# Queue order between attention and the first expert of a fused attention, mixture and SwiGLU kernel

## Chip, core and metric

The kernel runs on one core of a Trainium2 chip. The time is the device time of one execution in microseconds (us). The core has five engines that run beside each other, each from a queue of its own and in the order of that queue: TensorE (PE, matmuls and transposes into PSUM), VectorE (DVE), ScalarE (ACT), GpSimd (POOL, here mostly scatters to DRAM by computed row numbers) and SyncE (SP, here the queue that issues nearly all DMAs). An instruction waits for semaphores of other engines and of DMAs, and while it waits nothing behind it in its queue starts.

## What is computed

```python
attn = softmax(q k^T / 8 + slope[h] * -(i - j), masked to 0 <= i - j < 128) @ v   # 4 x 8 heads, 576 rows, 64 wide
x = attn as 2304 tokens x 512
logits = x @ w_gate + log1p(exp(x @ w_noise)) * noise                             # 8 experts
top2, top2_w = two largest logits of a token, softmax over the two
out[token] = sum over its two experts: top2_w * (relu(x @ w1[e]) @ w2[e])         # 512 -> 1024 -> 512
xn = out / rms(out) * rms_g
result = (silu(xn @ w_gate2) * (xn @ w_val)) @ w_out                              # 512 -> 1536 -> 512
```

## The kernel before

All arithmetic on PE that matters for precision is split: a float32 weight or activation becomes a float16 high part and a float16 rest, and three products replace one. A weight is split by an ACT instruction (the high part, L128, scaled) and a DVE instruction (the rest, L130), after a DMA of 512 KB has brought the float32 piece into one of four `st` buffers (L110).

**Attention.** The main loop counts `n`, one step for each pair of heads: 18 token tiles of 128 rows, four steps each, so n = 0 to 71, and some steps of run-out. A step issues the scores of n + 2 (L342), transposes of the probabilities of n, the product with v of n - 2. When a tile is complete, `split_x` makes its float16 halves `x16` (the high half on DVE L426, the rest on POOL L428, for the last tile on DVE), and `put_x` turns it into `xTg`: by a DMA transpose (L434) up to tile 14, by PE transposes (L438) and an ACT copy (L439) for tiles 15 to 17. `logits(t)` (L502) multiplies it with the gate weights. `route` then works on batches of tiles (0 to 2, 3 to 5, 6 to 9, 10 to 13, 14 and 15, 16 and 17): softplus on ACT (L512, L513), the top two on DVE, their rank by two small matmuls (L539, L541), and `slots` (L560), the row of each token in its expert's list. `scatter` sends the two copies of a tile's `x16` to `xrows` in DRAM by one indirect DMA each from POOL (L483), with a small memset ahead.

**Experts.** `row_steps` brings 128 rows of an expert's list back by a DMA transpose on SP (`xT`, L171). Expert 0 starts before the routing has ended: its first 256 rows when tiles 0 to 9 are routed, the next 128 after tile 13, and `LAST`, rows 384 to 639, after tile 17. `first_steps` is the hidden layer: for each of eight chunks f, 12 matmuls into a PSUM buffer (L187; names mm0, three buffers, and mm1, two), then ACT writes `hh` (L192) and DVE `hl` (L193), which frees the buffer. `second_steps` is the output layer, 24 matmuls of 512 columns a tile into `acc` (L208, two buffers), which ACT empties into `ys` (L230) for a DMA to `ybuf`. A generator yields after each six matmuls with the columns that PE has done.

**What sets the order.** Inside `manual_schedule` an engine's queue stands as the code is written. In the kernel before, this holds up to n = 75. From n = 76 up to the call of `drive` for expert 0 a scheduler of the framework orders the queues. From there on the order is by hand again: `drive` walks over PE's steps, counts columns, and calls a side generator when its due column is reached: `(start, period, generator)`. `weight_steps(e)` is such a generator: eight loads of 512 KB (four of w1, four of w2), each split in two halves. In the attention loop the loads and splits for expert 0 are called by a list of n. For expert 1 three loads stand directly ahead of `drive`.

```python
    drive(itertools.chain(exp0, expert_steps(0, LAST)),
          (0, 500, row_steps(0, LAST)), (0, 3000, weights0), (0, 3000, weights1),
          *((6000 + 6000 * i, 500, row_steps(1, cs)) for i, cs in enumerate(HALVES)),
          (40000, 4000, mix()), (58000, 5000, ahead(2)))
```

After expert 7 follow the combination, the norm and SwiGLU.

## Time and profile before

| | |
|---|---|
| three runs, median (lowest to highest) | 1026.11 us (1024.42 to 1030.59) |
| the profiled execution | 1031.71 us, of which the span from first to last instruction 1030.0 us |
| PE busy | 965.4 us, 94% of the span, 7184 matmuls |
| DVE, ACT, POOL busy | 685.8, 452.9, 215.2 us |
| mean granted clock of PE | 0.976 of full speed |
| chain that ended last, by engine | PE 70%, DMA 9%, DVE 9%, POOL 4% |

A share of the whole span says little here, since the program has stages with different limits: attention up to about 200 us, the hand-over to the experts up to about 250 us, experts to about 640 us, SwiGLU to the end. Times below are us from the start of the span.

### The profile page before, as it was taken

Reading aid. Unit: us, or ns where it says so; the run is one execution under the profiler, and the core shown is the slowest. Engines: PE = TensorE matmul, PEld = TensorE weight load, DVE = VectorE, ACT = ScalarE, POOL = GpSimd, SP = SyncE. Lnnn points to the kernel's source line nnn. Section 1 sums busy time; section 2 is a strip of 40 time slices with the busy share of each in tenths; the row PEclk is TensorE's granted clock in tenths of the full one; section 3 lists DMA queues with packets and bytes.
Section 4 is the critical chain, followed back from the end, with each engine's and each line's share of the span. In section 5 each row is a group of like instructions: output and inputs, shape, how many; then the busy total and the mean of one; then the engine's idle time right before and its main releaser. Section 6 shows DMA issues by size and latency. Waiting matters only on the chain.

```text
span 1030.0 us, 18541 instructions
## 1 busy us (share of the span) xinstructions
PE 965.4 (94%) x7184; PEld 672.3 (65%) x7184; DVE 685.8 (67%) x1584; ACT 452.9 (44%) x936; POOL 215.2 (21%) x261
## 2 busy tenths in 40 slices
PE   7898878869999999999999998889999999999997
PEld 4787777555565656565656577468658848857874
DVE  7788767533767666666666468998818936863750
ACT  6787766333445454545453244433422422341320
POOL 3446552600000000000000236652230150130000
PEclk9999998989999999999999999899999999999999
DMA  9999994783948584848582032302150151122000
GB/s 234 203 228 226 261 265 113 246 203 124 221 160 218 166 222 160 230 158 224 164 226 81 21 92 83 66 28 82 27 138 2 32 123 43 31 58 57 1 11 34
DMA packets 178560, 135.52 MB, mean 132 GB/s; under 512 B 130976, under 2 KB 148128, under 8 KB 178464
## 3 DMA queue, kind: packets, MB, share of 16 engines
q1 hardware_dynamic: 172704, 115.38, 44.3%
q0 software_dynamic: 5760, 18.88, 6.0%
q8 instruction: 58, 0.95, 0.4%
q14 instruction: 38, 0.31, 0.1%
HBM read 76.81 MB, written 26.74 MB: 101 GB/s over the span
## 4 chain that ended last, share of the span: by engine, by line
PE 70%; DMA 9%; DVE 9%; POOL 4%; issue 3%; ACT 3%; SPq 2%; ACTq 0%; DVEq 0%; POOLq 0%
PE mm L1045 20%; PE acc L208 19%; PE mm L187 18%; PE acc L972 11%; DMA raw<-in_qkv 3%; DVE sums L996 3%; POOL xrows L483 2%; DMA st<-in_moe_w 2%; DMA xTg<-x 1%; DMA xq<-xg 1%; DMA kqT<-kq 1%; POOL kq L267 1%; DVE ss L354 1%; SPq L901 1%; PE mm L342 1%
## 5 line engine op out<-in xcount | busy, mean ns | idle before, releaser
L187 PE MATMUL mm<-xT,w1h 128*128 128x256 f16 (+2 forms) x1088 | 167.2, 294 | 9.2 <-DVE hl L193 9.2
L187 PEld LDWEIGHTS <-w1h 128*128 128x128 f16 x1088 | 104.9, 99 | 48.6 <-issue 10.0
L193 DVE SCALAR_TENSOR_TENSOR hl<-mm,hh 128x256 f16<-128x256 f32 (+2 forms) x136 | 63.4, 469 | 104.4 <-ACT hh L192 102.6
L208 PE MATMUL acc<-w2h,hh 128*128 128x512 f16 x320 | 122.1, 382 | 0.0
L208 PE MATMUL acc<-w2l,hh 128*128 128x512 f16 x320 | 122.0, 381 | 0.0
L208 PE MATMUL acc<-w2h,hl 128*128 128x512 f16 x320 | 121.8, 381 | 0.0
L1002 POOL TENSOR_TENSOR sw<-sums,sw 128x256 f16<-128x256 f32 x36 | 28.5, 810 | 395.6 <-ACT sw L999 395.6
L208 PEld LDWEIGHTS <-hh 128*128 128x128 f16 x640 | 62.9, 98 | 72.9 <-ACT hh L192 0.6
L1045 PE MATMUL mm<-xq,sw 128*128 128x256 f16 x864 | 100.4, 273 | 1.7 <-DMA xq<-xg 1.7
L187 PE MATMUL mm<-xT,w1l 128*128 128x256 f16 (+2 forms) x544 | 92.7, 293 | 0.0
L1045 PEld LDWEIGHTS <-sw 128*128 128x128 f16 x864 | 84.4, 98 | 12.1 <-issue 2.0
L192 ACT ACTIVATE hh<-mm 128x256 f16<-128x256 f32 (+2 forms) x136 | 56.2, 418 | 80.2 <-PE mm L187 75.6
L972 PE MATMUL acc<-oh__3438,pgl 128*128 128x512 f16 (+2 forms) x228 | 84.5, 373 | 2.9 <-DVE pgl L954 2.9
L972 PE MATMUL acc<-oh__3438,pgh 128*128 128x512 f16 (+2 forms) x228 | 84.4, 372 | 0.2 <-ACT pgh L952 0.2
L972 PE MATMUL acc<-ol__3439,pgh 128*128 128x512 f16 (+2 forms) x228 | 84.3, 372 | 0.0
L972 PEld LDWEIGHTS <-pgh 128*128 128x128 f16 x456 | 44.4, 99 | 50.7 <-issue 2.2
L363 ACT ACTIVATE pr<-ss,nm 128x256 f32<-128x256 f32 (+1 forms) x144 | 63.1, 487 | 25.2 <-DVE nm L354 23.8
L187 PEld LDWEIGHTS <-w1l 128*128 128x128 f16 x544 | 52.7, 99 | 18.1
L354 DVE CUSTOM_DVE_ANT_0 ss<-mm,bias 128x256 f32<-128x256 f32 (+1 forms) x144 | 54.1, 396 | 11.4 <-PE mm L342 6.7
L371 PE MATMUL mm<-ident,pr 128*128 128x128 f32 x272 | 47.8, 293 | 14.0 <-DVE rs L416 8.8
L230 ACT ACTIVATE ys<-acc 128x512 f32<-128x512 f32 x40 | 23.7, 593 | 84.6 <-PE acc L208 68.6
L1054 DVE TENSOR_TENSOR gt<-mm,p 128x512 f32<-128x512 f32 x24 | 16.6, 690 | 60.7 <-PE mm L1045 58.6
(208 smaller groups left out, 1937.3 us busy)
## 6 DMA issues: line engine op xcount, KB each, us to landing
st<-in_moe_w SPq DMA_DIRECT2D x64, 512.0 KB, 5.0
ybuf<-ys SPq DMA_DIRECT2D x40, 256.0 KB, 2.0
raw<-in_qkv SPq DMA_DIRECT2D x17, 512.0 KB, 5.0
st<-in_moe_w_gate SPq DMA_DIRECT2D x12, 512.0 KB, 5.4
st<-in_moe_w_val SPq DMA_DIRECT2D x12, 512.0 KB, 4.9
st<-in_moe_w_out SPq DMA_DIRECT2D x12, 512.0 KB, 5.3
v<-in_qkv SPq DMA_DIRECT2D x18, 279.0 KB, 4.8
out<-ys SPq DMA_DIRECT2D x17, 256.0 KB, 2.2
```

The lines of the kernel that those rows point to most:

```text
L187: nc.tensor.matmul(hp[:, :w], w1[:, c, f * P:(f + 1) * P], xT[:, xo + c, cs], start=(n == 0), stop=(n == 3 * KC - 1))
L192: nc.scalar.activation(hh[:, f, hs], hp[:, :w], AF.Relu)
L193: nc.vector.scalar_tensor_tensor(hl[:, f, hs], hp[:, :w], 0.0, hh[:, f, hs], op0=OP.max, op1=OP.subtract)
L208: nc.tensor.matmul(yp, hx[:, f, i * P:(i + 1) * P], w2[:, f, :], start=(n == 0), stop=(n == 3 * FC - 1))
L230: nc.scalar.activation(ys, yp, AF.Copy, scale=YSC)
L354: nc.vector.tensor_tensor_reduce(out=d["ss"][:, j, c0:], in0=d["sp"][:, j, c0:], in1=bias[kind][:, 2 * d["hp"] + j, c0:], scale=-1.0 / KS, ...
L363: nc.scalar.activation(d["pr"][:, j, c0:], d["ss"][:, j, c0:], AF.Exp, scale=-1.0, bias=d["nm"][:, j:j + 1])
L371: nc.tensor.transpose(pt[:, j, kk, :], d["pr"][:, j, kk * P:(kk + 1) * P], ident)
L972: nc.tensor.matmul(op[:, ds], px[:, f, cs], w[:, f, ds], start=(k == 0), stop=(k == 3 * GC - 1))
L996: nc.vector.tensor_tensor(out=o, in0=x, in1=y, op=op)
L1002: nc.gpsimd.tensor_tensor(out=here[k][1], in0=x, in1=here[k][0], op=OP.subtract)
L1045: nc.tensor.matmul(pp, w(a, pa, c), xq[:, 4 * b + 2 * pb + c, :], start=(n == 0), stop=(n == 5))
```

## The change

The order is now by hand from the start of the loop to the end: `order.close()` at n = 76 is gone, and the steps of the run-out are written so that the queues stand as wanted. In its parts:

- `weight_steps` issues load i when the second half of piece i - 3 comes up, which is behind the split that last read the `st` buffer that it will fill. Before, it stood one half-step earlier.
- The batch of tiles 10 to 13 (`t0 = 10`) loses three pauses in `route` and is done three steps of n earlier. From n = 68 two scatters are issued in a step (before: from n = 77).
- The last tile is divided, split and turned one step earlier, its `logits` comes at n = 75 (before: 76), and the splits of expert 0's w2 are put behind that work (before: from n = 72 on).
- Expert 0 takes its first 256 and its next 128 rows through the hidden layer and then all three tiles through the output layer (before: hidden and output layer of the 256, then of the 128).
- The three loads for expert 1 ahead of `drive` are gone. Inside it, both transposes of `LAST` come at column 0, expert 1's weights from column 9000 every 2500 (before 0 and 3000), its rows from 14000 (before 6000).

```diff
@@ weight_steps
-        for i in range(len(srcs) + 3):
-            if i < len(srcs):
-                src = srcs[i]
-                sts.append(stage.tile([P, FE], F32, name="st").rearrange("p (a d) -> p a d", a=src.shape[1]))
-                nc.sync.dma_start(sts[i], src)
-            if i < 3:
-                yield
-                continue
...
+        def load():
+            src = srcs[len(sts)]
+            sts.append(stage.tile([P, FE], F32, name="st").rearrange("p (a d) -> p a d", a=src.shape[1]))
+            nc.sync.dma_start(sts[-1], src)
+
+        for _ in range(3):
+            load()
+            yield
...
+        for k, j in itertools.product(range(len(srcs)), range(2)):
+            if j and len(sts) < len(srcs):
+                load()
...
@@ drive
-                    next(s[2], None)
+                    if next(s[2], s) is s:
+                        break
@@ route (three places)
-            if t0 < 11:
+            if t0 < 10:
                 yield
@@ the loop over n
-        exp0 = itertools.chain(*(expert_steps(0, cs) for cs in EARLY.values()))
+        exp0 = expert_steps(0, *EARLY.values())
...
-            if n == 76:
-                order.close()
...
-            if n % 2 == 0 and HP <= n < NS + HP:
+            if n % 2 == 0 and HP <= n < NS + 2:
                 parts.append(divide((n - HP) // HP, (n - HP) // 2 % 2))
+            if n == NS + 1:
+                parts.append(divide(NT - 1, 1))
...
-                for _ in range(1 if n < 77 else 2):
-                    next(exp0, None)
+                next(exp0, None)
...
-            if p == (3 if NT - 6 <= t - 1 < NT - 1 else 2) and 1 <= t <= NT:
+            if p == (1 if t == NT else 3 if NT - 6 <= t - 1 < NT - 1 else 2) and 1 <= t <= NT:
                 split_x(t - 1)
...
-            if p == 3 and 1 <= t <= NT:
+            if p == (2 if t == NT else 3) and 1 <= t <= NT:
                 put_x(t - 1)
-            if n in (HP * NT + 1, HP * NT + 4) or p == 0 and 3 <= t < NT + 1:
-                r = {HP * NT + 1: NT - 2, HP * NT + 4: NT - 1}.get(n, t - 3)
+            if n in (NS + 1, NS + 3) or p == 0 and 3 <= t < NT + 1:
+                r = {NS + 1: NT - 2, NS + 3: NT - 1}.get(n, t - 3)
...
-                scatter(1 if n < 77 else 2)
-
-            for _ in range((n in (50, 53, 56, 58, 60, 62, 64, 66, 68, 70)) + (n in (72, 73) or n >= 76) * 2):
+                scatter(1 if n < 68 else 2)
+
+            if n in (50, 53, 56, 58, 60, 62, 64, 66, 68, 70, 72) or n > NS + 3:
                 next(weights0, None)
@@ ahead of drive for expert 0, and its call
-    for _ in range(3):
-        next(weights1)
...
-    order.enter_context(tc.manual_schedule())
...
-          (0, 500, row_steps(0, LAST)), (0, 3000, weights0), (0, 3000, weights1),
-          *((6000 + 6000 * i, 500, row_steps(1, cs)) for i, cs in enumerate(HALVES)),
+          (0, 0, row_steps(0, LAST)), (0, 1600, weights0), (9000, 2500, weights1),
+          *((14000 + 6000 * i, 500, row_steps(1, cs)) for i, cs in enumerate(HALVES)),
```

From expert 1's own matmuls on, the queues of all five engines hold the same instructions in the same order as before. Three places show what moves. Line numbers of the changed kernel differ by up to 3.

POOL's queue at the end of attention, before (x16_3047 is tile 16, x16_2048 and x16_2200 are tiles 10 and 11, whose scatters follow):

```order
L428 TENSOR_TENSOR x16_2744<-x_2628,x16_2744 128x512
L428 TENSOR_TENSOR x16_2895<-x_2773,x16_2895 128x512
L428 TENSOR_TENSOR x16_3047<-x_2937,x16_3047 128x512
L482 MEMSET apart_171 1x1
L483 DMA xrows_76<-x16_2048,slots_79 18432x1024
```

The same place after (x16_3065 is tile 16, x16_2411 and x16_2589 are tiles 12 and 13; the memset and the second scatter of each tile are left out):

```order
L431 TENSOR_TENSOR x16_2897<-x_2771,x16_2897 128x512
...
L486 DMA xrows_76<-x16_2048,slots_79 18432x1024
...
L486 DMA xrows_76<-x16_2200,slots_79 18432x1024
...
L486 DMA xrows_76<-x16_2411,slots_79 18432x1024
L431 TENSOR_TENSOR x16_3065<-x_2941,x16_3065 128x512
...
L486 DMA xrows_76<-x16_2589,slots_79 18432x1024
```

The rest of tile 16 (L428, now L431) stood ahead of all scatters of tiles 10 to 13, and now stands behind six of them.

SP's queue at the hand-over, before (xT_2794 are rows of expert 0, xT_3475 of expert 1; st_3428 to st_3432, st_3452 and st_3471 are expert 1's first five loads, st_3120 is expert 0's last; TENSOR_LOAD and ISA read a flag, and the x2 below them are the two transposes of `LAST`):

```order
L110 DMA st_3120<-in_moe_w2 128x2x512
L110 DMA st_3428<-in_moe_w1 128x4x256
L110 DMA st_3430<-in_moe_w1 128x4x256
L110 DMA st_3432<-in_moe_w1 128x4x256
L171 DMA_TRANSPOSE xT_2794<-xrows_76 128x8x128
L1157 TENSOR_LOAD over_82
L1157 ISA x2
L171 DMA_TRANSPOSE xT_2794<-xrows_76 128x8x128 x2
L110 DMA st_3452<-in_moe_w1 128x4x256
L231 DMA ybuf_77<-ys_3461 128x512
L110 DMA st_3471<-in_moe_w2 128x2x512
L171 DMA_TRANSPOSE xT_3475<-xrows_76 128x8x128 x3
```

The same place after (xT_2795 are rows of expert 0, xT_3506 of expert 1; st_3340 is expert 0's last load, st_3447 and the loads below it are expert 1's):

```order
L174 DMA_TRANSPOSE xT_2795<-xrows_76 128x8x128
L111 DMA st_3340<-in_moe_w2 128x2x512
L1156 TENSOR_LOAD over_82
L1156 ISA x2
L174 DMA_TRANSPOSE xT_2795<-xrows_76 128x8x128 x2
L111 DMA st_3447<-in_moe_w1 128x4x256
L111 DMA st_3472<-in_moe_w1 128x4x256
L111 DMA st_3504<-in_moe_w1 128x4x256
L174 DMA_TRANSPOSE xT_3506<-xrows_76 128x8x128 x3
L111 DMA st_3560<-in_moe_w1 128x4x256
```

All eight loads of expert 1 now stand behind the two transposes of `LAST` (five before), which wait for the last scatter.

ACT's queue where the hidden layer of `LAST` begins, before (w2h_3456 is expert 1's weight, st_3608 its last piece; hh_3680 is `LAST`):

```order
L128 ACTIVATE w2h_3456<-st_3542 128x512 x2
L230 ACTIVATE ys_3677<-acc_3644 128x512
L748 ACTIVATE cd_3441<-cd_3441 128x18
L192 ACTIVATE hh_3680<-mm0_3682 128x256
L128 ACTIVATE w2h_3456<-st_3608 128x512
L192 ACTIVATE hh_3680<-mm1_3701 128x256
```

The same place after (w1h_3533 and w2h_3535 are expert 1's weights, acc_3553, acc_3599 and acc_3643 the three output tiles of expert 0's first 384 rows, hh_3684 is `LAST`):

```order
L130 ACTIVATE w1h_3533<-st_3504 128x4x128 x2
L233 ACTIVATE ys_3596<-acc_3553 128x512
L130 ACTIVATE w1h_3533<-st_3560 128x4x128 x2
L130 ACTIVATE w2h_3535<-st_3574 128x512 x2
L130 ACTIVATE w2h_3535<-st_3592 128x512
L748 ACTIVATE cd_3372<-cd_3372 128x18
L233 ACTIVATE ys_3640<-acc_3599 128x512
L130 ACTIVATE w2h_3535<-st_3592 128x512
L130 ACTIVATE w2h_3535<-st_3614 128x512 x2
L130 ACTIVATE w2h_3535<-st_3626 128x512 x2
L233 ACTIVATE ys_3681<-acc_3643 128x512
L195 ACTIVATE hh_3684<-mm0_3686 128x256
```

All sixteen splits of expert 1's weights now stand ahead of the first `hh` of `LAST`. Before, the last two stood between its first ones.

## Rows read from the trace of the kernel before

**Rows 1.** Windows of 50 us: busy us and instructions by engine, clock, DMA share, GB/s.

```profile
150.00:200.00 50.00, 37.97 (x378) 30.64 (x376) 33.82 (x145) 25.46 (x55) 18.94 (x32) 0.86 0.66 189
200.00:250.00 50.00, 40.82 (x296) 26.48 (x295) 15.90 (x38) 15.01 (x37) 3.25 (x3) 0.90 0.69 169
250.00:300.00 50.00, 50.00 (x303) 29.42 (x301) 35.18 (x62) 23.97 (x47) 0.00 (x0) 1.00 0.67 181
```

**Rows 2.** Timeline of PE: start, us, instruction, idle time before it and its releaser.

```profile
158.72 0.28 PE L502 MATMUL rt<-wgh,xTg 128*128 128x16 f16 x4 [7.42 <-DMA xTg<-x]
...
174.74 0.73 PE L438 MATMUL mm<-ident,x 128*128 128x128 f16 x8
...
176.23 0.60 PE L187 MATMUL mm<-xT,w1h 128*128 128x256 f16 x4
...
177.54 0.25 PE L502 MATMUL rt<-wgh,xTg 128*128 128x16 f16 x4
...
193.23 0.25 PE L502 MATMUL rt<-wgh,xTg 128*128 128x16 f16 x4
...
216.37 0.58 PE L187 MATMUL mm<-xT,w1h 128*128 128x128 f16 x4 [6.78 <-DVE hl L193]
...
223.52 0.60 PE L187 MATMUL mm<-xT,w1h 128*128 128x256 f16 x4
...
232.64 0.94 PE L187 MATMUL mm<-xT,w1h 128*128 128x256 f16 x4 [2.40 <-DVE hl L193]
```

**Rows 3.** The chain that ended last, in order of time: start, us, what.

```profile
203.09 3.42 DMA xrows<-x,slots
...
228.58 1.15 ACT w2h L128 x2
...
238.39 10.36 PE acc L208 x48
```

**Rows 4.** Timeline of ACT at the start of the last rows of expert 0.

```profile
230.22 0.37 ACT L192 ACTIVATE hh<-mm 128x256 f16<-128x256 f32 x1
```

**Rows 5.** Timeline of SP, which issues the DMAs: start, us that the issue took.

```profile
146.29 0.81 SPq L110 DMA_DIRECT2D st<-in_moe_w  x1
147.21 3.55 SPq L434 DMA_TRANSPOSE xTg<-x  x1
...
165.56 18.71 SPq L110 DMA_DIRECT2D st<-in_moe_w  x6
...
230.67 1.65 SPq L110 DMA_DIRECT2D st<-in_moe_w  x3
```

**Rows 6.** Windows as in Rows 1, of four stretches.

```profile
150.00:155.00 5.00, 1.30 (x13) 1.14 (x10) 2.44 (x9) 0.98 (x3) 0.00 (x0) 0.92 1.24 313
160.00:165.00 5.00, 5.00 (x37) 4.71 (x36) 3.21 (x20) 3.38 (x9) 0.00 (x0) 0.55 0.58 123
...
206.50:230.50 24.00, 16.96 (x152) 12.62 (x150) 7.54 (x18) 7.35 (x22) 0.00 (x0) 0.86 0.94 208
232.00:237.50 5.50, 4.86 (x30) 3.72 (x30) 3.17 (x9) 1.49 (x5) 0.00 (x0) 0.69 0.91 285
```

**Rows 7.** Timeline of DVE: step 69, then the slots of two batches.

```profile
171.70 0.08 DVE L354 DVE_READ_ACCUMULATOR2_ANT nm<- 128x1 f32 x1
...
176.60 0.21 DVE L557 TENSOR_TENSOR oh<-oh,rt 128x64 f32<-128x64 f32 x1
...
177.10 0.17 DVE L560 SCALAR_TENSOR_TENSOR slots<-chosen,rank 128x8 int32<-128x8 f32 x1
...
196.72 0.16 DVE L560 SCALAR_TENSOR_TENSOR slots<-chosen,rank 128x4 int32<-128x4 f32 x1
```

**Rows 8.** Timeline of POOL: tile 16's rest, first and seventh scatter behind it.

```profile
173.87 1.16 POOL L428 TENSOR_TENSOR x<-x,x 128x512 f16<-128x512 f32 x1 [6.11 <-DVE x L426]
...
177.54 0.98 POOL L483 DMA_INDIRECT xrows<-x,slots  x1 [2.48 <-DVE rank L562]
...
186.28 0.96 POOL L483 DMA_INDIRECT xrows<-x,slots  x1 [0.22 <-issue]
```

More of the change, by code (lines that the diff above doesn't have):

```diff
@@ L105, in weight_steps @@
         sts, last = [], None
-        for i in range(len(srcs) + 3):
-            if i < len(srcs):
-                src = srcs[i]
-                sts.append(stage.tile([P, FE], F32, name="st").rearrange("p (a d) -> p a d", a=src.shape[1]))
-                nc.sync.dma_start(sts[i], src)
-            if i < 3:
-                yield
-                continue
-            if i == 3:
-                ws += [wpool.tile([P, KC, FE], F16, name="w1h"), wpool.tile([P, KC, FE], F16, name="w1l"),
-                       wpool.tile([P, FC, DM], F16, name="w2h"), wpool.tile([P, FC, DM], F16, name="w2l")]
-            k = i - 3
-            for j in range(2):
-                fs = slice(j * n // 2, (j + 1) * n // 2)
-                if k < 4:
-                    st = sts[k][:, :, fs]
-                    hi, lo = (w[:, :, k * n + fs.start:k * n + fs.stop] for w in ws[:2])
-                else:
-                    st = sts[k][:, j:j + 1]
-                    hi, lo = (w[:, (k - 4) * m + j:(k - 4) * m + j + 1] for w in ws[2:])
-                scale = SW1 if k < 4 else SW2
-                nc.scalar.activation(hi, st, AF.Copy, scale=scale)
-                if last:
-                    nc.vector.scalar_tensor_tensor(*last, op0=OP.mult, op1=OP.subtract)
-                last = lo, st, scale, hi
-                yield
@@ new lines, in load @@
+        def load():
[5 more added lines that the diff above has]
+            yield
+        ws += [wpool.tile([P, KC, FE], F16, name="w1h"), wpool.tile([P, KC, FE], F16, name="w1l"),
+               wpool.tile([P, FC, DM], F16, name="w2h"), wpool.tile([P, FC, DM], F16, name="w2l")]
+        for k, j in itertools.product(range(len(srcs)), range(2)):
+            if j and len(sts) < len(srcs):
+                load()
+            fs = slice(j * n // 2, (j + 1) * n // 2)
+            if k < 4:
+                st = sts[k][:, :, fs]
+                hi, lo = (w[:, :, k * n + fs.start:k * n + fs.stop] for w in ws[:2])
+            else:
+                st = sts[k][:, j:j + 1]
+                hi, lo = (w[:, (k - 4) * m + j:(k - 4) * m + j + 1] for w in ws[2:])
+            scale = SW1 if k < 4 else SW2
+            nc.scalar.activation(hi, st, AF.Copy, scale=scale)
+            if last:
+                nc.vector.scalar_tensor_tensor(*last, op0=OP.mult, op1=OP.subtract)
+            last = lo, st, scale, hi
+            yield
@@ L534, in route @@
             yield
-            if t0 < 11:
+            if t0 < 10:
                 yield
@@ L554, in route @@
             yield
-            if t0 < 11:
+            if t0 < 10:
                 yield
```

## The prediction

> **What bounds the kernel now.** First the windows of 50 us. From 250 us on PE is busy 50.00 of 50 us [rows 1], and the queues there stand as before, so a change can come only from the stretch before. Between 150 and 250 us PE is busy 37.97 + 40.82 = 78.8 of 100 us: 21.2 us of idle time are all that there is to win, with what the clock takes. The timeline of PE tells where they lie [rows 2]: 7.42 us up to 158.72, where `logits` of tile 13 waits for its DMA transpose `xTg`; 6.78 us up to 216.37 and 2.40 us up to 232.64, where the hidden layer of expert 0 waits for `hl`. Behind an idle time the granted clock is low: 0.55 between 160 and 165 us [rows 6].
>
> Who is late in the second half is seen in the chain that ended last, read forwards [rows 3]: the last scatter is issued at 203.09 and lands at 206.51. Only then can SP turn the rows of `LAST`, and all loads behind that in SP's queue come later still. The chain ends with two splits of expert 1's w2 on ACT at 228.58, right behind a load; the first `hh` of `LAST` follows at 230.22 [rows 4]; PE starts again at 232.64 and ends expert 0 at 238.39 + 10.36 = 248.75. So from 206.51 to 232.64 the hand-over is paced by transfers and by ACT's queue behind them, and PE fills in. Whatever the change does, the end of expert 0 follows from two numbers: when the last scatter lands, and how long the transfers ahead of `LAST`'s first `hh` then take.
>
> **The change part by part.** *A load behind a transpose.* Load 3 of expert 0 is issued at 146.29, directly ahead of tile 13's `xTg` at 147.21 [rows 5], for which PE waits 7.42 us. It now stands behind it. The load is 128 x 4 x 256 x 4 bytes = 0.524 MB; at the 313 GB/s of 150 to 155 us [rows 6] that is 1.7 us. Bounds: 0, if the scatters fill the place (the DMA share is 1.24 there), and 2.5 at the 208 GB/s of the later stretch [rows 6]. I take -1.7, the row of the place itself. For experts 2 to 7 the same edit changes no row of SP's queue: nothing.
>
> *The batch of tiles 10 to 13 earlier.* Its `slots` now stand directly behind the maxima of step 69, which end at 171.78; from L557 at 176.60 to the end of `slots` at 177.27 the work takes 0.67 us [rows 7]. So they come at 171.78 + 0.67 - 1.7 = 170.75, 6.5 us earlier than before. But POOL's queue has six of the eight scatters ahead of tile 16's rest. The first scatter started 0.27 us behind `slots`, the seventh 8.74 us behind the first (177.54, 186.28) [rows 8]: 170.75 + 0.27 + 8.74 = 179.8, plus 1.16 for the rest [rows 8] = 180.9. PE wants it for the second half of tile 16's transposes at 174.74 + 0.36 - 1.7 = 173.4 [rows 2]. Before, POOL did it at 173.87, with nothing ahead. The change thus adds a wait of 7.5 us on PE, and behind it in PE's queue stand the last products with v, expert 0's first matmuls and `logits` of tiles 15 to 17; at 0.96 busy + 0.3 us for a scatter it is 6.4. Behind such a wait the clock is low: the 2.75 us from the transposes' middle to the end of tile 15's `logits` (175.10 to 177.85 [rows 2]) may take twice as long; I take half of that, 1.4. `Logits` of tile 15 end at 180.9 + 2.75 + 1.4 = 185.1, against 177.85.
>
> *The last tile, freed of the splits of w2.* Before, from there to the `slots` of tiles 16 and 17 (196.88 [rows 7]) it took 19.0 us, with w2's splits between. A bare route takes 3.65 us (193.23 to 196.88 [rows 2, 7]). Now: 2.7 us of the first route to its rank matmuls, some 2 us of DVE work on tile 17 between (an estimate: about five operations of the size in these rows), then on PE half a chunk, the transposes, a chunk and `logits`, 0.65 + 0.73 + 1.31 + 0.31 = 3.0 (chunk: 176.23 to 177.54, transposes 0.73 [rows 2]), then the second route with half a chunk, a split and two `hl` between, 3.65 + 1.65. That is 13.0 us, 6 less than before: `slots` at 198.1. The last of four scatters starts 0.27 + 3 x 1.26 behind, at 202.2, or at 202.8 with the spacing of 8.74 / 6; it lands 3.42 us later [rows 3], at 205.6 to 206.2, against 206.51. I take -0.5. So what the splits gave up, POOL's wait has taken. Bounds: -7, if that wait doesn't come, and +1.4, if the whole stretch runs at half clock.
>
> *Three loads behind the last scatter.* Before, SP issued expert 1's first three loads among the six between 165.56 and 184.27 [rows 5], while little else moved. Now they stand behind the two transposes of `LAST`, which wait for the last scatter, and ahead of five transposes and five loads that stood there already. Three such loads in a row, issued at 230.67 [rows 5], fill the window from 232 to 237.5: 5.5 us at 285 GB/s [rows 6]. Between 206.5 and 230.5 us the DMA share is 0.94 [rows 6], so some 24 x 0.06 = 1.4 us of it fits into pauses: +4.1 us. Bounds: 0, if the share hides slack, and 1.57 MB at 208 GB/s = 7.5. This counts in full, since ACT now has all sixteen splits of expert 1 ahead of the first `hh` of `LAST`, and PE has five buffers, five chunks, before it must wait. That two splits moved ahead of that `hh` costs nothing more: DVE had them ahead of `hl` before.
>
> The Trainium skill, DMA: Bandwidth & Descriptors, section Rules for kernel authors, says to issue a DMA early, compute, and wait for it late. It speaks against this part: by it the loads stay where they were, and the 4.1 us are the price of moving them. By the opposite, that PE has enough else to do, the part costs 0 and the sum below would be -0.5, so 1025.6. The rows stand nearer to the rule, as the next paragraph shows.
>
> *PE's own work.* With 384 rows in the hidden layer first, PE has 8 x 1.31 + 8 x 0.65 = 15.7 us there and three output tiles of 10.36 / 2 = 5.2 us: 15.5. From 182 us, with 2.5 us of low clock and 3 us of waits for rank and `x16`, it has done the hidden layer at some 205, the output at 221, and five chunks of `LAST` at 227 to 229 (the third output tile waits some 2 us, since the `ys` of the first stands behind six splits). But `hh` of `LAST` comes at 230.22 - 0.5 + 4.1 = 233.8. The 6.78 us wait goes, the 2.40 us wait becomes 5 to 6: PE's gain is given back.
>
> *At no cost:* the order by hand in place of the scheduler, the `break` in `drive`, the later start of expert 1's rows (they stand behind its loads, and PE needs them at 252).
>
> **Sum.** The two numbers of the first part: landing -0.5 (the 1.7 of the first edit is in it), transfers +4.1. Expert 0 ends at 248.75 + 3.6 = 252.4, and all behind it shifts alike: span 1033.6, that execution 1035.3. The profiled execution of before (1031.71) lies 5.6 us over the median, so I add the difference to the median: 1026.11 + 3.6 = 1029.7 us.
>
> **The rivals.** *Faster.* POOL's wait is shorter, or the transfers flow together. For it: POOL's spans are rough, and the DMA moved 313 GB/s at 150 us. Against it: the order of POOL's queue, and PE's transposes that wait for it. With the landing at 199.5 the sum is -7 + 4.1 = -2.9; with the three loads in pauses as well -7: 1019. To win more than 1% the last scatter would have to land by 196 with the loads at nothing; PE's own work alone would allow that (221 + 10.5 + 10.4 - 7 = 235), the transfers hardly.
>
> *Slower.* ACT's queue ahead of `LAST`'s first `hh`: it runs no `hh` until the eighth load of expert 1 has landed. With 7.5 us for the three loads, the landing at +1.4, and PE idle so long that the three chunks left of the hidden layer (3.9 us) run at half clock, about +2, the sum is +10.9: 1037. It decides from the point where the eighth load lands some 8 us later than before. For it: between 206.5 and 230.5 us only 208 GB/s moved, since transposes and loads alternate. Against it: plain loads in a row moved 285.
>
> *It does little.* The edit of `weight_steps` changes no queue after the hand-over, and the two new waits could just weigh up the old ones: 0 within 2 us, 1026.
>
> **How the numbers follow.** Chances: forecast, +1 to +8 us, 0.52; faster, -2 to -8, 0.20; little, within 2 us, 0.14; slower, +8 to +12, 0.14. The range reaches over all of these but their ends: -7 to +11, 1019 to 1037, which leaves about 0.15 out. About 1%, 10.3 us, is what a measurement of this kernel can tell from no change. Of the faster case a third of its chance lies beyond that, with surprises 0.07; of the slower case most, 0.13; within 1% is 0.80.
>
> **What the changed profile would show.** Right: PE's wait for tile 13's `xTg` at 5 to 6 us; tile 16's rest on POOL 8 to 9 us behind the first scatter of its batch, and PE waiting 6 to 7.5 us at the transposes there; the last scatter landing at 205 to 207; expert 1's first load issued right behind `LAST`'s transposes at 208 to 209; PE waiting 4 to 7 us within `LAST`'s hidden layer with ACT on a load of expert 1 ahead; expert 1's first matmul at 251 to 254. Wrong: no wait of PE at tile 16, a landing before 200, or `hh` of `LAST` running when PE gets there; then it is faster. A wait of over 10 us in `LAST` makes it the slower case.

## The result, and the profile after

The changed kernel takes 1035.85 us (median of ten runs, 1032.14 to 1039.15) against 1027.2 us of the kernel before (ten runs, 1024.42 to 1030.86): a ratio of 1.0082, with a 95% interval of 1.0062 to 1.0102. It is slower by some 8.6 us. The forecast was slower by 3.6 us, 1029.7, in a range up to 1037. The two profiled executions, 1035.65 and 1031.71, are 3.9 us apart, close to the forecast. So two questions are left: whether that agreement comes from the steps of the prediction, and where the other 4.7 us between the medians come from.

The timeline of PE in the changed kernel (start, us, instruction, idle time before it and its releaser) answers [rows 2]:

```profile
154.54 0.26 PE L505 MATMUL rt<-wgh,xTg 128*128 128x16 f16 x4 [1.84 <-DMA xTg<-x]
...
163.03 0.40 PE L441 MATMUL mm<-ident,x 128*128 128x128 f16 x4 [2.39 <-DVE x L429]
...
179.81 0.61 PE L441 MATMUL mm<-ident,x 128*128 128x128 f16 x4 [6.36 <-POOL apart L485]
...
207.69 0.38 PE L190 MATMUL mm<-xT,w1h 128*128 128x128 f16 x4 [1.59 <-DVE hl L196]
...
225.70 0.60 PE L190 MATMUL mm<-xT,w1h 128*128 128x256 f16 x4
...
236.29 1.01 PE L190 MATMUL mm<-xT,w1h 128*128 128x256 f16 x4 [3.88 <-DVE hl L196]
```

PE's wait for tile 13 has gone from 7.42 to 1.84 us, and the one of 6.78 us in the hidden layer to 1.59. Two are new or longer: 6.36 us at the second half of tile 16's transposes (L441), and 3.88 us instead of 2.40 within `LAST`.

The timeline of POOL answers [rows 8]. Six scatters now stand ahead of tile 16's rest (L431), which was done at 173.87 before:

```profile
171.06 0.99 POOL L486 DMA_INDIRECT xrows<-x,slots  x1 [6.82 <-DVE rank L565]
...
177.60 0.96 POOL L486 DMA_INDIRECT xrows<-x,slots  x1 [0.22 <-issue]
...
178.58 1.17 POOL L431 TENSOR_TENSOR x<-x,x 128x512 f16<-128x512 f32 x1
...
202.79 0.96 POOL L486 DMA_INDIRECT xrows<-x,slots  x1 [0.22 <-issue]
```

The `slots` of two batches on DVE answer [rows 7]: those of tiles 10 to 13 come 6.5 us earlier, those of the last tiles 1.4 us later.

```profile
170.61 0.17 DVE L563 SCALAR_TENSOR_TENSOR slots<-chosen,rank 128x8 int32<-128x8 f32 x1
...
198.10 0.16 DVE L563 SCALAR_TENSOR_TENSOR slots<-chosen,rank 128x4 int32<-128x4 f32 x1
```

SP, which issues the DMAs, answers [rows 5]: the two transposes of `LAST`, directly behind them the first three loads of expert 1, then three transposes of expert 1's rows, and only at 220.04 the fourth load.

```profile
208.16 2.60 SPq L174 DMA_TRANSPOSE xT<-xrows  x2
210.86 1.63 SPq L111 DMA_DIRECT2D st<-in_moe_w  x3
212.54 7.40 SPq L174 DMA_TRANSPOSE xT<-xrows  x3
220.04 0.52 SPq L111 DMA_DIRECT2D st<-in_moe_w  x1
```

ACT at the hand-over answers [rows 4]. It waits for load after load, and the first `hh` of `LAST` runs at 235.08, against 230.22:

```profile
215.94 0.63 ACT L130 ACTIVATE w1h<-st 128x512 f16<-128x512 f32 x1 [6.43 <-DMA st<-in_moe_w]
...
223.99 1.15 ACT L130 ACTIVATE w1h<-st 128x512 f16<-128x512 f32 x2 [3.52 <-DMA st<-in_moe_w]
...
228.93 1.15 ACT L130 ACTIVATE w2h<-st 128x512 f16<-128x512 f32 x2 [3.78 <-DMA st<-in_moe_w]
...
235.08 1.47 ACT L195 ACTIVATE hh<-mm 128x256 f16<-128x256 f32 x5
```

The chain that ended last answers [rows 3]: the last scatter lands at 202.79 + 5.35 = 208.14 (206.51 before), and expert 0 ends at 252.25 (248.75 before).

```profile
202.79 5.35 DMA xrows<-x,slots
...
241.89 10.36 PE acc L211 x48
252.25 15.60 PE mm L190 x96
```

The windows, to [rows 1, 6]: in the middle of the hand-over PE is now busy 22.50 of 24 us, 16.96 before. PE does more of its work there, and still expert 0 ends later, since the first `hh` of `LAST` comes later.

```profile
206.50:230.50 24.00, 22.50 (x152) 13.36 (x152) 9.07 (x20) 8.39 (x21) 0.00 (x0) 1.00 0.92 225
```

Behind expert 0 nothing has changed: from its end to the end of the span it is 1030.0 - 248.75 = 781.25 us before, and 1033.8 - 252.25 = 781.55 after.

### The profile page after: what moved, and what is told of

It is laid out like the page before. It is cut to its first block, busy times and chain, and to the rows that moved or that the text cites. A ratio compares the mean times of both kernels' runs of the same rounds, so it can differ in the third digit from the quotient of the medians.

```text
span 1033.8 us, 18539 instructions
## 1 busy us (share of the span) xinstructions
PE 965.0 (93%) x7184; PEld 671.7 (65%) x7184; DVE 688.0 (67%) x1584; ACT 454.1 (44%) x936; POOL 213.9 (21%) x261
## 4 chain that ended last, share of the span: by engine, by line
PE 69%; DVE 11%; DMA 9%; issue 3%; POOL 3%; ACT 2%; SPq 2%; DVEq 0%; ACTq 0%; POOLq 0%
PE mm L190 19%; PE acc L211 19%; PE mm L1044 18%; PE acc L971 11%; DMA kqT<-kq 3%; DVE sums L995 2%; DMA raw<-in_qkv 2%; DMA st<-in_moe_w 2%; DVE ss L357 1%; POOL xrows L486 1%; DMA xq<-xg 1%; PE acc L401 1%; PE mm L374 1%; PE mm L345 1%; SPq L900 1%
## 5 line engine op out<-in xcount | busy, mean ns | idle before, releaser
L233 ACT ACTIVATE ys<-acc 128x512 f32<-128x512 f32 x40 | 23.7, 593 | 75.8 <-PE acc L211 67.3
```

The costliest lines, as they stand in the source:

```text
L233: nc.scalar.activation(ys, yp, AF.Copy, scale=YSC)
```

## The experiments

Twelve runs, on three chips, which are told apart here by their numbers, 13, 7 and 8; each ratio is to runs of the kernel before on the same chip, while the chip of the first comparison (the ten runs of each kernel above) is not on record. Where a gain in us is worked out from ratios it can differ by up to 1 us from the difference of the medians. The "rest" of tile 16 is its second float16 half (L431).

| kernel | chip | median, us | before there, us | ratio (95% interval) |
|---|---|---|---|---|
| pool_rest | 13 | 1036.63 | 1031.76 | 1.0046 (1.0027 to 1.0066) |
| loads_first | 13 | 1033.71 | 1031.76 | 1.0022 (1.0000 to 1.0044) |
| both | 13 | 1032.28 | 1031.76 | 1.0002 (0.9979 to 1.0024) |
| after_again | 7 | 1035.83 | 1031.61 | 1.0041 (1.0022 to 1.0060) |
| batch_back | 7 | 1029.76 | 1031.61 | 0.9989 (0.9968 to 1.0010) |
| both_rows_late | 7 | 1029.46 | 1031.61 | 0.9984 (0.9966 to 1.0002) |
| weights_only | 7 | 1028.92 | 1031.61 | 0.9968 (0.9954 to 0.9983) |
| weights_spaced | 8 | 1028.46 | 1026.73 | 1.0014 (0.9999 to 1.0030) |
| weights_rows_late | 8 | 1019.96 | 1026.73 | 0.9932 (0.9912 to 0.9952) |
| batch_back_both | 8 | 1019.64 | 1026.73 | 0.9922 (0.9902 to 0.9941) |
| pool_rest_again | 8 | 1028.59 | 1025.87 | 1.0027 (1.0005 to 1.0048) |

The kernel before takes 1031.6 to 1031.8 us on two of the chips and 1025.9 to 1026.7 on the third. The first comparison has 1027.2.

**Before, a second profile** (chip 13; no edit).

> The kernel before, unchanged, for a second profile. The two profiled executions differ by 3.9 us (1031.71 before, 1035.65 after), the medians of ten by 8.65 us (1027.2, 1035.85). Theory: the profiled execution of before was one of its long ones, and it lost the 4 to 5 us ahead of 250 us, in the stretch that the change rewrites. Then a second profile ends expert 0 (last matmul of its output layer) at 243 to 246 us instead of 248.75, and its time is 1025 to 1029. Rival: it ends expert 0 at 248 to 250 again and what is left is lost or won behind, in the experts or SwiGLU; or the time is 1031 again.

It took 1034.12 us, and expert 0 ended at 250.82: the theory fell. The length of the hand-over repeats: the last scatter lands at 206.53 + 3.71 = 210.24, the first `hh` of `LAST` runs at 233.96, 23.72 us later (23.71 in the first profile). But ahead of it there is something that the rows of the first profile hardly showed. PE's and ACT's timelines, in the train of eight scatters of tiles 10 to 13 (176.48 to 185.38):

```profile
185.06 0.27 PE L187 MATMUL mm<-xT,w1h 128*128 128x256 f16 x1 [1.04 <-issue]
...
187.92 0.60 PE L187 MATMUL mm<-xT,w1h 128*128 128x256 f16 x2 [1.16 <-issue]
```

```profile
188.01 0.18 ACT L512 ACTIVATE ex<-rt 128x16 f32<-128x16 f32 x1 [4.38 <-remote]
```

PE stops between matmuls of one group, and the trace names nothing that they wait for; ACT stops for 4.38 us, though the `logits` that it needs (tile 15's) were done at 177.16. "issue" and "remote" are the trace's words for having found no releaser in the program. Such a stop is called a standstill below.

**Tile 16's rest on DVE** (the changed kernel; chip 13).

```diff
-            lo = nc.gpsimd if t < NT - 1 else nc.vector
+            lo = nc.gpsimd if t < NT - 2 else nc.vector
```

> The changed kernel, with the rest of tile 16 on DVE instead of POOL, so that it no longer stands behind six scatters. Theory (this wait is what took the gain of the earlier batch and of the freed last tile): PE's wait of 6.36 us at the second half of tile 16's transposes falls under 1 us, the slots of tiles 16 and 17 come 6 to 8 us earlier (190 to 192 instead of 198.1), the last scatter lands at 200 to 202 instead of 208.1, expert 0 ends 5 to 8 us earlier, 244 to 247; time 5 to 8 us under the changed kernel, 1028 to 1031. Rival (the transfers for expert 1 and ACT's queue behind them set the hand-over, whenever the last scatter lands): the wait goes and the scatter lands earlier, but expert 0 ends less than 2.5 us earlier; time 1033 to 1036.

The wait of 6.36 us went, as both expected, and nothing was gained: 1.0046. But not for the rival's reason, since the last scatter hardly started earlier (202.18, against 202.79). This profiled run, 1032.07, is the shortest of its twelve (median 1036.63), and in it expert 0 ends at 249.75, 2.5 us earlier than in the changed kernel. The standstill now lies where the wait was. ACT and DVE resume together, and PE waits behind them:

```profile
182.16 0.18 ACT L515 ACTIVATE ex<-rt 128x16 f32<-128x16 f32 x1 [3.91 <-remote]
```

```profile
182.32 0.16 DVE L419 TENSOR_SCALAR rs<-acc 128x4 f32<-128x4 f32 x1 [3.00 <-remote]
```

```profile
183.59 0.25 PE L505 MATMUL rt<-wgh,xTg 128*128 128x16 f16 x4 [3.81 <-DVE nl L520]
```

**Three loads ahead of the transposes of `LAST`** (the changed kernel; chip 13).

```diff
-          (0, 0, row_steps(0, LAST)), (0, 1600, weights0), (9000, 2500, weights1),
+          (0, 1600, weights0), (8000, 0, itertools.islice(weights1, 3)), (8000, 0, row_steps(0, LAST)),
+          (16500, 2500, weights1),
```

> The changed kernel, with the first three loads of expert 1's weights again ahead of the two transposes of the last rows on SP; the splits and the other five loads stay where they were. Theory (these three loads behind the last scatter cost 4.1 us): the first splits of expert 1 on ACT no longer wait for a load (6.43 us in the changed kernel), the first hh of the last rows comes 3 to 5 us earlier (230 to 232 instead of 235.08), PE's wait of 3.88 us there goes, expert 0 ends 3.5 to 5.5 us earlier; time 1030 to 1033. Rival (the three loads were hidden, the other five and the transposes between them set the pace): less than 1.5 us of change. A third way: the loads slow the scatters, which land later, and the gain is given back.

The third way happened. From the transposes of `LAST` to its first `hh` it is 234.77 - 211.77 = 23.0 us, 4 us less than in the changed kernel (26.9). But these transposes come 7.0 us behind the start of the last scatter (204.76) instead of 5.4, as the loads move beside it. The ratio is 1.0022, some 2 us under after_again's 1.0041, which the intervals do not separate.

```profile
204.76 0.96 POOL L486 DMA_INDIRECT xrows<-x,slots  x1 [0.22 <-issue]
```

```profile
211.77 6.64 SPq L174 DMA_TRANSPOSE xT<-xrows  x5
```

**Both edits** (chip 13).

> Both edits, the rest of tile 16 on DVE and the three loads ahead of the transposes of the last rows. Theory: the two waits are in a row (one sets when the last scatter lands, the other how long the transfers behind it take), so the gains add: expert 0 ends 9 to 12 us earlier than in the changed kernel, 240 to 243; time 1024 to 1027, level with before or up to 0.3% under it. Rival (PE's own work or the transfers are the bound behind the first 6 us): the gain is that of the better single edit, and no more than 2 us over it.

1.0002: level with before, but the gains did not add. Expert 0 ends at 238.23 + 10.36 = 248.59, which is 3.7 us earlier than in the changed kernel (9 to 12 expected), 1.2 us earlier than in pool_rest and 1.8 us earlier than in loads_first, so the rival's figure holds. Its reason, PE's own work or the transfers, is only half of it: PE waits 4.66 us in the standstill, and 3.86 us in `LAST`.

**The changed kernel again** (chip 7; no edit).

> The changed kernel once more, so that its distance to before and to the other variants is measured on one chip. Theory (the ten runs against ten of the first comparison are right, and the forecast of +3.6 us was too small): ratio 1.006 to 1.010 again. Rival (the forecast's size is right, and the first comparison was off by the scatter of single runs): 1.002 to 1.005. In the profile, PE's wait at the second half of tile 16's transposes is 6 to 6.5 us again, and the first hh of the last rows comes 26 to 28 us behind the landing of the last scatter (26.9 in the first profile, 23.7 in both profiles of before).

1.0041, the rival's figure. The changed kernel's time is what it was (1035.83, 1035.85); before is 4.4 us longer here than in the first comparison. PE's wait at tile 16 is 5.49 us, a little under what was expected, and from landing to `hh` it is 234.60 - (202.94 + 3.51) = 28.15 us, a little over.

**The batch of tiles 10 to 13 where it was** (the changed kernel; chip 7).

```diff
-            if t0 < 10:
+            if t0 < 11:
...
-                scatter(1 if n < 68 else 2)
+                scatter(1 if n < 77 else 2)
```

> The changed kernel with the batch of tiles 10 to 13 where it was: the three pauses of its routing are back, and two scatters a step from n = 77 only. The rest of tile 16 then stands ahead of all scatters of the batch, on POOL as before. Two questions. First, the time: theory (the earlier batch alone made POOL's wait): the wait goes, and the kernel is as the one with tile 16's rest on DVE, 1.003 to 1.006 of before; rival (the earlier batch is worth something of its own): slower than that by 3 us or more, 1.007 and up. Second, the stretch of 4 to 5 us in which ACT, DVE and PE stood still at once while the scatters of the batch ran (pool_rest, both, before_again: it began 5 to 7 us behind the first scatter). Theory (it goes with the scatters): it now begins at 180 to 184, 5 to 7 us behind the first scatter at 175 to 178. Rival (it goes with the place in the program): it stays at the logits of tiles 15 and 16, at 175 to 179.

0.9989: 5.2 parts in a thousand under after_again on the same chip, 5.4 us. Neither figure: undoing the batch gains more than freeing tile 16's rest alone. The last scatter starts at 197.02 instead of 202.94. The standstill is there (PE stops for 3.83 us from 177.54), but `logits` of tile 16 run at 174.33, ahead of it, and in pool_rest at 183.59, behind it. That this is the reason is not shown by a run of its own. The question about the standstill was put badly: the first scatter starts at 171.63 here, 1.7 us later than in after_again, so a place in the program and the scatters can't be told apart by it.

**Expert 1's transposes behind its loads** (the kernel with both edits; chip 7).

```diff
-          *((14000 + 6000 * i, 500, row_steps(1, cs)) for i, cs in enumerate(HALVES)),
+          *((42000 + 6000 * i, 500, row_steps(1, cs)) for i, cs in enumerate(HALVES)),
```

> The kernel with both edits (tile 16's rest on DVE, three loads of expert 1 ahead of the last rows' transposes), and the five transposes of expert 1's rows put behind all of expert 1's loads on SP. Theory (the hand-over is paced by SP's queue, in which transposes stand between the loads that ACT waits for): ACT's waits of 7.9 and 3.5 us for loads fall to under 2 us each, the first hh of the last rows comes 4 to 7 us earlier (224 to 227 instead of 230.5 in the kernel with both edits), PE's wait of 3.86 us goes and with it the low clock behind it, expert 0 ends 4 to 7 us earlier; ratio to before 0.993 to 0.997. Rival (the loads themselves, or the buffers that the splits must free first, pace it): less than 1.5 us, ratio 0.9985 to 1.001.

The mechanism is as expected: the first `hh` of `LAST` comes 226.59 - 209.75 = 16.84 us behind its transposes, against 230.51 - 207.83 = 22.68, and PE waits for nothing in `LAST`. SP and ACT with both edits, where three of the five instructions are expert 1's transposes, ahead of the fourth load:

```profile
207.83 6.64 SPq L174 DMA_TRANSPOSE xT<-xrows  x5
```

```profile
230.51 1.47 ACT L195 ACTIVATE hh<-mm 128x256 f16<-128x256 f32 x5
```

and here, with loads in their place:

```profile
209.75 2.59 SPq L174 DMA_TRANSPOSE xT<-xrows  x2
212.44 2.39 SPq L111 DMA_DIRECT2D st<-in_moe_w  x3
```

```profile
226.59 0.65 ACT L195 ACTIVATE hh<-mm 128x256 f16<-128x256 f32 x2
```

The chain has `LAST` and expert 1 without a pause:

```profile
223.45 10.48 PE mm L190 x96
233.93 10.36 PE acc L211 x48
244.29 15.60 PE mm L190 x96
```

The ratio, 0.9984, is a smaller gain than expected (0.993 to 0.997): it lies only 1.9 us under that of the kernel with both edits, on another chip, and the intervals do not separate the two.

**The order of the weight loads alone** (the kernel before, with the new `weight_steps` and no other edit: SP's queue changes by a few places, ACT's, DVE's and POOL's not at all; chip 7).

> The kernel before with the new order of the weight loads alone, which moves SP's queue by a few places and no other queue. The prediction put this at -1.7 us (0, if the scatters fill the place, to -2.5). Theory: PE's wait for tile 13's transpose falls from 4.4 to 7.4 us (two profiles of before) to 2 us or less, as in the changed kernel (1.84), but the next waits, on DVE for tile 15's halves and on POOL for its rest, take most of it: ratio 0.997 to 1.000. Rival: the whole of the wait comes back, ratio 0.993 to 0.996.

0.9968, 3.3 us faster than before: the good end of the theory (0.997), and the interval reaches from 1.8 to 4.7 us. PE's wait for tile 13 is gone; 1.90 us for tile 15's halves and 0.83 for its rest follow.

**Scatters further apart** (weights_only; chip 8).

```diff
                 nc.gpsimd.memset(apart, 0)
+                for _ in range(4 if 10 <= t < 14 else 0):
+                    nc.gpsimd.memset(wide, 0)
```

> The kernel before with the new order of the weight loads (weights_only), and four memsets of 128 x 256 words on POOL ahead of each scatter of tiles 10 to 13, so that these scatters start further apart (1.26 us now). In nine profiles, PE's gaps of over 0.4 us that wait for nothing lie only within a train of eight scatters, from about 5 us behind its first to 2.5 us behind its last, with ACT and DVE standing still beside. Theory (a dense train does this): with 2 us and more from one scatter to the next, the gaps from 180 to 187 us (seven of 0.4 to 1.2 us in weights_only) shrink to under 1 us in all and ACT's standstill of 4.4 us goes; the train ends later (190 to 194), so the time is about that of weights_only, 0.995 to 0.999 of before. Rival (each scatter stops the engines for a piece, however far apart): the gaps sum to as much, over a longer stretch. Second rival (a place in the program, not the scatters): they stay at 180 to 187 as they are.

The question stays open: the scatters start 2.6 us apart, and no gap is to be seen; but neither is one in any other profile of chip 8, where they start 1.26 us apart. The time, 1.0014, misses the expected 0.995 to 0.999. Two other things are shown. The longer train costs PE 3.89 us at the rows of expert 0 that wait for it. And the wait for tile 13 can come back with the load out of its way:

```profile
156.74 0.28 PE L507 MATMUL rt<-wgh,xTg 128*128 128x16 f16 x4 [6.87 <-DMA xTg<-x]
```

It is 6.87 us here, and under 2 us in the eleven other profiles with the new load order. Why it came back is not shown.

**weights_only, with expert 1's transposes behind its loads** (chip 8).

```diff
-          *((6000 + 6000 * i, 500, row_steps(1, cs)) for i, cs in enumerate(HALVES)),
+          *((28000 + 6000 * i, 500, row_steps(1, cs)) for i, cs in enumerate(HALVES)),
```

> weights_only, with the five transposes of expert 1's rows behind all of expert 1's loads on SP. Theory (transposes between the loads pace the hand-over, in the kernel before too): in the kernel with both edits the same move brought the first hh of the last rows from 22.7 us behind the issue of their transposes to 16.8 us; here it comes at 226 to 229 instead of 232.2, PE's wait of 2.21 us in the last rows goes and the half clock behind it, expert 0 ends 3 to 5 us earlier; ratio to before 0.992 to 0.995. Rival (ACT's wait of 7.8 us for the fourth load of expert 1, which stands behind the transposes of the last rows either way, sets it): 0.995 to 0.998.

0.9932, the theory's figure. PE still waits 6.70 us while ACT waits for the fourth load of expert 1, which is the rival's objection, but from there it runs through:

```profile
208.18 0.59 PE L189 MATMUL mm<-xT,w1h 128*128 128x128 f16 x4 [6.70 <-DVE hl L195]
```

```profile
217.04 0.38 ACT L194 ACTIVATE hh<-mm 128x256 f16<-128x256 f32 x1 [0.67 <-PE mm L189]
```

ACT now waits for PE there, where it had PE waiting. The first `hh` of `LAST` comes 217.04 - 198.34 = 18.7 us behind its transposes, against 23.7 in before and 23.5 in weights_only. How much of the ratio is due to this edit is not separated, since weights_only was timed on chip 7.

**The changed kernel without its three costs** (the edits of batch_back, loads_first and both_rows_late together; chip 8).

> The changed kernel with its three costs taken out: the batch of tiles 10 to 13 where it was, three loads of expert 1 ahead of the last rows' transposes, and expert 1's five transposes behind its loads. What is left of the change is the order of the weight loads, the last tile ahead of w2's splits, and expert 0's first 384 rows in one piece. Theory (what is left is worth 3 us for the load order and 3 us or more for the last tile): ratio 0.990 to 0.994, below weights_only (0.9968). Rival (the last tile ahead of the splits gains nothing, since the scatters set when the last one lands): 0.995 to 0.998.

0.9922, 8 us faster than before on chip 8 (7.1 by the medians) and 16 under both medians of the changed kernel. It is level with weights_rows_late within the intervals, so these runs don't show that the earlier last tile is worth anything beside the other two edits. In the window behind 200 us PE has no idle time left, at a granted clock of 1.00:

```profile
200.00:250.00 50.00, 50.00 (x302) 29.45 (x301) 22.92 (x44) 23.27 (x47) 0.00 (x0) 1.00 0.74 190
```

**Tile 16's rest on DVE, on the other chip** (the kernel of pool_rest; chip 8).

> The changed kernel with tile 16's rest on DVE, once more. On one chip, where before takes 1031.7 us, this edit gained nothing (1.0046 against 1.0041 for the changed kernel), and all profiles there show a standstill of PE, ACT and DVE of 3 to 6 us within the train of scatters in which the wait on POOL lay; on another, where before takes 1026.7 us, three profiles show none. The changed kernel takes 1035.85 and 1035.83 us on a chip of each kind. Theory (the standstill lies under POOL's wait and takes its place where the chip has it; it also made before 4 to 5 us longer there, and the changed kernel not): on a chip where before takes 1026 to 1028 us, the profile shows no such gaps, the edit gains the whole wait, 5 to 8 us, ratio 1.000 to 1.003; on a chip where before takes 1031 to 1033 us, gaps again and 1.003 to 1.006. Rival (the wait on POOL costs nothing on any chip, since the transfers set the hand-over): where before takes 1026 to 1028 us, no gaps, and still 1.006 to 1.010.

1.0027, inside the theory's figure; 1028.59 us, 7.3 us under the changed kernel's two medians, 8 under the same kernel on chip 13. The profile has no standstill. `ex` runs as soon as `logits` are there, and the last scatter starts at 195.60 instead of 202.18:

```profile
176.26 0.18 ACT L515 ACTIVATE ex<-rt 128x16 f32<-128x16 f32 x1
```

```profile
195.60 1.23 POOL L486 DMA_INDIRECT xrows<-x,slots  x1 [0.21 <-issue]
```

Expert 0 ends at 247.32, which is 4.9 us earlier than in the first profile of the changed kernel and 2.4 us earlier than in pool_rest. This profiled run, 1031.03, is the longest of its twelve, and that of pool_rest the shortest, so the two profiles show less than the 8 us between the medians. By these figures the wait on POOL costs the changed kernel 5 to 7 us where there is no standstill. That is read across chips, because the changed kernel itself was not timed on chip 8.

## Why the prediction was right in its steps and short in its size

**The queues: right.** The prediction's times, each followed by that of the profile after: `slots` of tiles 10 to 13 at 170.75, done 170.78; the rest's end at 180.9, 179.75; PE's wait at tile 16 6.4 to 7.5, 6.36; `logits` of tile 15 done at 185.1, 185.03; `slots` of the last tiles at 198.1, 198.10; the last scatter's start at 202.2 to 202.8, 202.79; the end of expert 0 at 252.4, 252.25; that execution at 1035.3, 1035.65. One row was misread: the end of tile 15's `logits` in before, taken as 177.85, is 177.99, which moves the sum by 0.1 us.

**The load behind the transpose, -1.7 us: too small.** Alone it is worth 3.3 us (weights_only). I priced the load's own transfer at 313 GB/s; what went was 4.4 to 7.4 us of waiting (the two profiles of before), of which DVE and POOL at tile 15 took 1.90 and 0.83 us back.

**The landing, -0.5 us: too good by 2 us in that profile.** The last scatter started as forecast but took 5.35 us to land, not 3.42. In three more profiles with the same queues around it, it took 2.73 (pool_rest), 3.51 (after_again) and 5.18 us (pool_rest_again): the term was taken from one row, and such rows scatter by 2.6 us.

**Three loads behind the last scatter, +4.1 us: right as an interval.** Landing to first `hh` went from 23.7 (twice) to 26.9 and 28.15, +3.8 on average. Undone, it gave 4 us back there and lost some 3 of them at the scatter's landing (7.0 us, against 4.2 on the mean of the four profiles with the loads behind it). What the prediction did not see is that the transposes between the loads cost more than the loads' place: 5.8 us of the interval (22.68 to 16.84), and that before paid for this too (23.7, against 18.7 in weights_rows_late).

By the rule of the Trainium skill that the prediction named (DMA: Bandwidth & Descriptors, section Rules for kernel authors), the loads were to be issued early. The runs agree for the interval. They add that three loads beside a scatter that others wait for made it land 6.7 to 7.2 us behind its start (four kernels), against 2.7 to 5.4 without.

**The sum: near for the profiles, in part by luck, and short for the medians.** Between the two profiles expert 0 ends 3.5 us later, where the forecast had 3.6. But the terms missed and made up for each other: the landing came 1.6 us later instead of 0.5 earlier, landing to `hh` grew by 3.2 us instead of 4.1, and from that `hh` to PE's start in `LAST` it took 236.29 - 235.08 = 1.21 us instead of 232.64 - 230.22 = 2.42.

The step that failed is the last one, "The profiled execution of before (1031.71) lies 5.6 us over the median, so I add the difference to the median". The profiled execution of the changed kernel is the first of its ten timed runs and lies at the median of both its sets (1035.85, 1035.83). That of before is not among its ten, lies above all of them (at most 1030.86), and lies at the median of chips 13 and 7 (1031.6 to 1031.8). A difference of 4 us can't be carried over from such a pair.

What the traces show to differ is the standstill. All eight profiles of chips 13 and 7 have PE stops of 0.4 us and more without a releaser, all of them between the start of a train of eight scatters and 2.5 us behind its last; none of the four of chip 8 has one, nor the first of the changed kernel. The profile of before has them in its first train:

```profile
142.51 0.26 PE L502 MATMUL rt<-wgh,xTg 128*128 128x16 f16 x4 [1.01 <-issue]
...
144.86 0.19 PE L404 MATMUL acc<-vl,ph 128*128 128x64 f16 x1 [0.67 <-issue]
```

and in its second ACT stops twice, 1.85 and 1.35 us, without a releaser. The traces differ in a second way, and split alike. The view of the DMAs has a time from issue to landing for the scatters in the profile after and in the four of chip 8, and none in the nine others, here before and after:

```profile
xrows<-x,slots POOLq DMA_INDIRECT x36
```

```profile
xrows<-x,slots POOLq DMA_INDIRECT x36, 5.4
```

In those nine traces 9 to 10% of the records of DMA completions are missing, in the five under 1%. So the two profiles of the first comparison are of two kinds, and their difference mixes the change with the kind.

How much that is can be read where two kernels have the same queues. Up to the transposes of `LAST` weights_only (chip 7) and weights_rows_late (chip 8) have; the last scatter starts at 204.92 in the one and at 194.69 in the other. For pool_rest it is 202.18 on chip 13 and 195.60 on chip 8. These are differences of single profiles, 10.2 and 6.6 us, and larger than the 4 to 6 us between the medians of before. The clock does not explain the chips' difference: among the runs of before with a mean granted clock of 0.978 to 0.982 the medians are 1031.8 us (chip 13), 1031.6 (chip 7) and 1026.6 and 1027.2 (two sets on chip 8).

The reading that fits these figures: where the chip has the standstill, before loses 4 to 5 us (1031.7 against 1026 to 1027), and the changed kernel, which waits for POOL in the same stretch, loses nothing (1035.83, 1035.85). So its loss is 4.2 us on the one kind of chip, near the forecast, and twice that in the first comparison.

This link is argued, not shown. That the first comparison's runs of before had no standstill is inferred from their median (1027.2) alone; no profile of before was taken on chip 8, and the changed kernel was not timed there. And batch_back, which takes POOL's wait out on a chip with the standstill, gains 5.4 us there, where pool_rest gains nothing.

**The rivals.** "POOL's wait is shorter" fell (6.36 us); "ACT's queue ahead of `LAST`'s first `hh`" was the mechanism, at the forecast's size and not at the rival's. Of the marks of the last part, five missed: PE's wait for tile 13 at 1.84 instead of 5 to 6 us, that in `LAST` at 3.88 instead of 4 to 7, tile 16's rest 7.5 us behind the first scatter instead of 8 to 9, the landing at 208.14 instead of 205 to 207, and expert 1's first load at 210.86 instead of 208 to 209; PE's wait at tile 16 and expert 1's first matmul hold.

## What to carry to other kernels

Work that is moved earlier goes in front of something: ask what stands behind it on the same in-order queue, here one subtraction of 1.2 us behind six scatters. Before a difference of profiles is added to a median, look where the profiled run lies among the timed ones; if it lies outside, the two profiles may not be of one kind, and the stretch that makes the difference has to be found first. And at a hand-over sort the queue of transfers by who waits first: five transposes that PE needed only some 30 us later stood between loads, and moving them took 5.8 us out of the wait for the first `hh`.

## What the runs showed of the hardware

- During trains of eight scatters from POOL (256 KB each, 1.26 us apart) PE stops without a releaser in the trace, for 0.4 to 3.8 us at a time, in all eight profiles of two chips and in the first of before, from about 5 us behind the first scatter to 2.5 us behind the last. Beside it, ACT's or DVE's longest stop without a releaser is 3.5 to 6.7 us in the second train of six of these profiles. The trace names no cause, and on the third chip the same queues show none. The cause is open. The traces that show it also lack 9 to 10% of the DMA completions, so it may even have to do with the recording. Spacing the scatters was not tried where the standstill is.
- The kernel before takes 1031.7 us on those two chips and 1026 to 1027 on the third. The standstill and the missing completions are the differences that the profiles of the variants show.
- POOL's row of a scatter ends after 0.96 us in most rows; the last scatter lands 2.7 to 7.2 us behind its start. The Trainium skill (Perfetto Trace Analysis, section DMA Instruction — SWDGE (GPSIMD)) says that the profiler's end is that of the descriptors, not of the data; these rows agree.
